# Heads of odd pairs swapped, level 32 on eighths of the array, nine attention phases for thirteen, and one PSUM bank for the first dense product, in a fused linear-attention and MLP kernel

## Chip, cores and metric

One core of a Trainium2 chip. The metric is the device time of one execution in microseconds (us), median over several executions.

Short names in the text: PE is TensorE (the matmul engine), DVE is VectorE, ACT is ScalarE, SP the engine that issues most transfers. PSUM is the memory that matmuls write to; it has eight banks. A quarter of PE's array is 64 rows by 64 columns, an eighth 64 rows by 32 columns. "Changed kernel" is the kernel after the change.

## The reference

A recurrent attention (per head a 48x48 state that decays by `w` and takes up `k v`), followed by a dense block with `h - tanh(h)` between two matrix products:

```python
batch, n_heads, seq, head_dim = (4, 8, 768, 48)
for t in range(S):
    cur = np.einsum('bhd,bhe->bhde', u[None] * kt, vt)
    y[:, :, t] = np.einsum('bhd,bhde->bhe', rt, state + cur)
    state = wt[:, :, :, None] * state + np.einsum('bhd,bhe->bhde', kt, vt)
# x = y as (B*S, 384)
h = x @ w_in            # 384 -> 2048
g = h - np.tanh(h)
return g @ w_out        # 2048 -> 384
```

## The kernel before

The 3072 tokens are cut into eight blocks of 384. Each block's dense part has 16 steps (one per 128 columns of the hidden layer): three matmuls into `hp`, then `h`, `tanh` and a correction series on ACT and DVE, and three steps later three matmuls into `acc`. While the dense steps of block i run, the attention of block i+1 runs between them, one *phase* in a step. Two heads make a pair: head 0 of a pair lies on partitions 0 to 47, head 1 on 64 to 111. Inside a chunk of 64 tokens, scores are computed in levels 1, 2, 4, 8, 16, 32; `update` forms the state at each chunk's start; `result` adds a state part (state times r) and a value part (scores times v).

The dispatch of phases and of the work ahead of them:

```python
        def phase(self, ps, k):
            if k < 2:
                self.level_1(ps, HALVES[k])
                if k == 1:
                    self.decay(1, 0, NPAIR, ("rp",))
            elif k < 7:
                self.level(ps, 2 ** (k - 1), 0, NPAIR)
            elif k < 11:
                p0 = HALVES[(k - 7) // 2]
                if k % 2 == 1:
                    self.turn(ps, p0)
                else:
                    self.update(ps, p0)
            elif k < 13:
                self.result(ps, HALVES[k - 11])
                if k == 12:
                    self.fill_holes([nc.sync])

        def prepare(self, k):

            if k == 10:
                for name, src in (("rmix", rT), ("kmix", kT), ("wt", wT), ("kq", kT)):
                    self.load(name, src, 0, NPAIR)
            elif k == 13:
                self.load("rp", rT, 0, NPAIR)
                self.load_v()
                self.mix(0, NPAIR, False)
                for m in (1, 2, 4, 8, 16, 32):
                    self.totals(m, 0, NPAIR)
            elif k == 14:
                self.decay(1, 0, NPAIR, ("kq",))
```

The result, with its fence between the two parts:

```python
        def result(self, ps, p0, holes_full=False):

            St, rp = states[self.q], self.tiles["rp"]
            yp = ps.tile([P, 2, BANK], F32, name="att", tag="att")
            for p in range(UP):
                for c in range(NCP):
                    for par in range(2):
                        for h in range(2):
                            rows = slice(64 * h, 64 * h + D)
                            t0 = (p0 + p) * NB + (2 * c + par) * L
                            n0 = (p * NCP + c) * L
                            nc.tensor.matmul(yp[64 * h:64 * h + 64, par, n0:n0 + L],
                                             lhsT=St[rows, p0 + p, 2 * c + par, :],
                                             rhs=rp[rows, t0:t0 + L],
                                             start=(p == 0 and c == 0), stop=False,
                                             skip_group_check=True)

            nc.tensor.drain().then_inc(fence, 1)
            fences.append(None)
            nc.tensor.wait_ge(fence, len(fences))
            for p in range(UP):
                for c in range(NCP):
                    for h in range(2):
                        for par in range(2):
                            toks = slice(64 * par, 64 * par + 64)
                            e0 = (p0 + p) * D2 + h * D
                            n0 = (p * NCP + c) * L
                            nc.tensor.matmul(yp[64 * h:64 * h + D, par, n0:n0 + L],
                                             lhsT=self.v[toks, c, e0:e0 + D],
                                             rhs=A[toks, h, p0 + p, c, :],
                                             start=False, stop=(p == UP - 1 and c == NCP - 1),
                                             skip_group_check=True)
            for p in reversed(range(UP)):
                i = p0 + p
                src = yp[:, :, p * NCP * L:(p + 1) * NCP * L].rearrange("e a (c t) -> e c a t", t=L)
                dst = self.xT[:, i, :] if i < KC else self.late
                dst = dst.rearrange("e (c a t) -> e c a t", a=2, t=L)
                for rows in (slice(0, D), slice(64, 64 + D)) if holes_full else (slice(0, P),):
                    nc.scalar.copy(out=dst[rows], in_=src[rows])
```

A level (level 32 is `m == L // 2`; `gram` is a loop of 48 small matmuls, two heads x two halves of the output, so on four quarters of the array):

```python
        def level(self, ps, m, p0, n):
            gr = self.gram(ps, self.tiles["kq"], self.tiles["rp"], p0, n, m, L // 2)
            self.decay(m, p0, n)
            nb = L // (2 * m)
            if m == L // 2:

                for par in range(2):
                    rows = slice(64 * par, 64 * par + 32)
                    dst = A[rows, :, p0:p0 + n].rearrange("s h p c t -> s h (p c) t")
                    nc.scalar.copy(out=dst[:, :, :, 32:],
                                   in_=gr[rows].rearrange("s h (n t) -> s h n t", t=32))
                return
            for h in range(2):
                dst = A[:, h, p0:p0 + n].rearrange("s p c (b two m) -> s (p c) b two m",
                                                   two=2, m=m)[:, :, :, 1, :]
                src = gr[:, h].rearrange("s (n b m) -> s n b m", b=nb, m=m)
                mask = masks[m].bitcast(U8).unsqueeze(1).to_broadcast([P, n * NCP, nb, m])
                nc.vector.copy_predicated(out=dst, mask=mask, data=src)
```

The dense product and the main loop (cut at ...):

```python
    def first(xT, f, ps):
        hp = ps.tile([P, NB], F32, name="hp", tag="hp", bufs=2)
        for kc in range(KC):
            nc.tensor.matmul(hp, lhsT=w_in_sb[:, f, kc, :], rhs=xT[:, kc, :],
                             start=(kc == 0), stop=(kc == KC - 1))
        ...

        for i, blk in enumerate(blocks):
            here = xT
            later = blocks[i + 1] if i + 1 < len(blocks) else None
            after = blocks[i + 2] if i + 2 < len(blocks) else None
            if later:
                xT = later.begin()
            second = Second(blk.b * S + blk.q * NB, ps_d)
            for f in range(NF):
                g, next_rest = first(here, f, ps_d)
                waiting.append((second, f, g))

                for n, op in enumerate(rest):
                    op()
                    if n >= 2 and extra:
                        extra.pop(0)()
                for op in extra:
                    op()
                rest = next_rest
                if later:
                    later.phase(ps_a, f)
                extra = convert(*raws.pop(0)) if raws else []
                if after:
                    after.prepare(f)
                if len(waiting) > LAG:
                    s, fs, gs = waiting.pop(0)
                    s.add(fs, gs)
                if i == 0 and f + AHEAD + RAWS < NF:
                    raws.append(load_weights(f + AHEAD + RAWS, nc.gpsimd))
```

Of the kernel before, what the change touches and what calls it, by code (L numbers as in the profile page):

```python
# [44 lines left out]
P = 128  # L46
L = 64
# [33 lines left out]
def kernel(  # L81
# [88 lines left out]

    fence, fences = tc.alloc_semaphore("fence"), []

    class Block:


        def __init__(self, b, q):
            self.b, self.q = b, q
            self.cols = slice(q * NB, (q + 1) * NB)
            self.tiles = {}
            self.tots = {}  # L180

# [18 lines left out]
        def mix(self, p0, n, copies):  # L200
# [5 lines left out]
            for t, src, odd in ((kmix, kq, 1), (rmix, rp, 0)):  # L206
                if copies:
                    nc.vector.tensor_copy(out=part(t, p0, n, 1 - odd), in_=part(src, p0, n, 1 - odd))
                for p in range(p0, p0 + n):
                    nc.scalar.activation(out=part(t, p, 1, odd),  # L210
                                         in_=part(src if copies else t, p, 1, odd),
                                         func=AF.Copy, scale=u_sb[:, p:p + 1])

        def gram(self, ps, lhs, rhs, p0, n, m, width):

            ps_t = ps.tile([P, 2, BANK], F32, name="att", tag="att")
# [47 lines left out]
        def level(self, ps, m, p0, n):  # L264
            gr = self.gram(ps, self.tiles["kq"], self.tiles["rp"], p0, n, m, L // 2)
            self.decay(m, p0, n)
            nb = L // (2 * m)
            if m == L // 2:

                for par in range(2):  # L270
                    rows = slice(64 * par, 64 * par + 32)
                    dst = A[rows, :, p0:p0 + n].rearrange("s h p c t -> s h (p c) t")
                    nc.scalar.copy(out=dst[:, :, :, 32:],
                                   in_=gr[rows].rearrange("s h (n t) -> s h n t", t=32))
                return
# [6 lines left out]

        def turn(self, ps, p0):

            ks = work.tile([P, UP, NCP, P], F32, name="ks", tag="ks")
            tp = ps.tile([P, 2, BANK], F32, name="att", tag="att")
# [6 lines left out]
            self.ks = ks  # L293

        def update(self, ps, p0):

            ks, last = self.ks, self.q == NQ - 1
            kvp = ps.tile([P, 2, BANK], F32, name="att", tag="att")
# [23 lines left out]
        def result(self, ps, p0, holes_full=False):  # L322

            St, rp = states[self.q], self.tiles["rp"]
            yp = ps.tile([P, 2, BANK], F32, name="att", tag="att")
            for p in range(UP):
                for c in range(NCP):
                    for par in range(2):
                        for h in range(2):
                            rows = slice(64 * h, 64 * h + D)  # L330
                            t0 = (p0 + p) * NB + (2 * c + par) * L
                            n0 = (p * NCP + c) * L
                            nc.tensor.matmul(yp[64 * h:64 * h + 64, par, n0:n0 + L],  # L333
                                             lhsT=St[rows, p0 + p, 2 * c + par, :],
                                             rhs=rp[rows, t0:t0 + L],
                                             start=(p == 0 and c == 0), stop=False,
                                             skip_group_check=True)
# [4 lines left out]
            for p in range(UP):  # L342
                for c in range(NCP):
                    for h in range(2):
                        for par in range(2):
                            toks = slice(64 * par, 64 * par + 64)
                            e0 = (p0 + p) * D2 + h * D
                            n0 = (p * NCP + c) * L
                            nc.tensor.matmul(yp[64 * h:64 * h + D, par, n0:n0 + L],  # L349
                                             lhsT=self.v[toks, c, e0:e0 + D],  # L350
                                             rhs=A[toks, h, p0 + p, c, :],
                                             start=False, stop=(p == UP - 1 and c == NCP - 1),
                                             skip_group_check=True)
            for p in reversed(range(UP)):
                i = p0 + p
                src = yp[:, :, p * NCP * L:(p + 1) * NCP * L].rearrange("e a (c t) -> e c a t", t=L)
                dst = self.xT[:, i, :] if i < KC else self.late
                dst = dst.rearrange("e (c a t) -> e c a t", a=2, t=L)
                for rows in (slice(0, D), slice(64, 64 + D)) if holes_full else (slice(0, P),):
                    nc.scalar.copy(out=dst[rows], in_=src[rows])  # L360
# [10 lines left out]
        def phase(self, ps, k):  # L371
            if k < 2:
                self.level_1(ps, HALVES[k])
                if k == 1:
                    self.decay(1, 0, NPAIR, ("rp",))
            elif k < 7:
                self.level(ps, 2 ** (k - 1), 0, NPAIR)
            elif k < 11:
                p0 = HALVES[(k - 7) // 2]
                if k % 2 == 1:  # L380
                    self.turn(ps, p0)
                else:
                    self.update(ps, p0)
            elif k < 13:
# [190 lines left out]
```

## Time and profile before

| before | value | how to read it |
|---|---|---|
| time | 713.07 us, median of the 3 runs known before the prediction (710.51 to 714.27); a fourth came with the result | span of the profiled run 710.4 us, about 2 us less than its time |
| PE, DVE, ACT busy | 95%, 79%, 69% of the span | averages over boot, block 0 and the rest, which have different bounds |
| boot, to the first dense matmul | 48.74 us | a chain through several engines |
| block 0 | 99.81 us | DVE also converts the weights |
| blocks 1 to 6 | 489.34 us, 81.5 to 81.6 each | PE bound |
| block 7 with the end | 72.51 us | no attention beside it |

The borders are the starts of the first `hp` matmul of each block in PE's order of work. The lines behind these numbers are in the prediction below.

### The profile page before, as it was taken

Reading aid. Unit: us, or ns where it says so; the run is one execution under the profiler, and the core shown is the slowest. Engines: PE = TensorE matmul, PEld = TensorE weight load, DVE = VectorE, ACT = ScalarE, POOL = GpSimd, SP = SyncE. Lnnn points to the kernel's source line nnn. Section 1 sums busy time; section 2 is a strip of 40 time slices with the busy share of each in tenths; the row PEclk is TensorE's granted clock in tenths of the full one; section 3 lists DMA queues with packets and bytes.
Section 4 is the critical chain, followed back from the end, with each engine's and each line's share of the span. In section 5 each row is a group of like instructions: output and inputs, shape, how many; then the busy total and the mean of one; then the engine's idle time right before and its main releaser. Section 6 shows DMA issues by size and latency. Waiting matters only on the chain.

```text
span 710.4 us, 19979 instructions
## 1 busy us (share of the span) xinstructions
PE 675.0 (95%) x8480; PEld 434.6 (61%) x8480; DVE 560.7 (79%) x1125; ACT 487.1 (69%) x957; POOL 10.9 (2%) x32
## 2 busy tenths in 40 slices
PE   4876899999999999999999999999999999999997
PEld 3754555666666666656666666656666566665554
DVE  7778999689876897679876898579976898656774
ACT  4348479586767667586676757686676867677875
POOL 2010000000000000000000000000000000000000
PEclk9987799999999999999999999999999999999999
DMA  8377332213013401114013310124012000000000
GB/s 328 109 266 272 136 128 89 80 43 134 3 47 86 157 14 46 54 36 169 2 46 88 119 52 2 51 82 168 2 46 88 2 35 2 5 7 34 0 0 35
DMA packets 30841, 54.37 MB, mean 77 GB/s; under 512 B 2336, under 2 KB 28704, under 8 KB 30752
## 3 DMA queue, kind: packets, MB, share of 16 engines
q1 hardware_dynamic: 25424, 38.15, 16.3%
q0 software_dynamic: 1872, 10.22, 4.0%
q10 hardware_dynamic: 3456, 4.72, 1.8%
q8 instruction: 67, 1.10, 0.6%
q14 instruction: 22, 0.18, 0.1%
HBM read 47.19 MB, written 4.72 MB: 73 GB/s over the span
## 4 chain that ended last, share of the span: by engine, by line
PE 65%; PEld 11%; DVE 10%; issue 8%; ACT 2%; DMA 2%; PEldq 1%; SPq 1%; ACTq 0%; DVEq 0%
PE acc L471 27%; PE hp L433 25%; PE att L230 10%; PEld hp L433 4%; PEld acc L471 3%; PEld att L333 2%; DVE w_sb L168 2%; PEldq L339 1%; DVE w_sb L166 1%; DVE hs L450 1%; DVE states L318 1%; PE att L349 1%; PE att L290 1%; PE att L308 1%; DMA rp<-in_rT 1%
## 5 line engine op out<-in xcount | busy, mean ns | idle before, releaser
L471 PE MATMUL acc<-w_sb,gT 128*128 128x384 f32 x768 | 279.9, 501 | 0.0
L433 PE MATMUL hp<-xT,w_sb 128*128 128x384 f32 x768 | 273.8, 493 | 3.0 <-DMA xT<-late 3.0
L433 PEld LDWEIGHTS hp<-xT,w_sb 128*128 128x128 f32 x768 | 147.8, 193 | 106.9 <-issue 5.4
L471 PEld LDWEIGHTS acc<-w_sb,gT 128*128 128x128 f32 x768 | 139.9, 191 | 84.4 <-issue 2.3
L440 ACT ACTIVATE h<-hp 128x384 f32<-128x384 f32 x128 | 62.2, 486 | 170.7 <-PE hp L433 168.1
L455 DVE TENSOR_TENSOR th<-h,th 128x384 f32<-128x384 f32 x128 | 70.9, 554 | 56.0 <-ACT th L444 56.0
L450 DVE SCALAR_TENSOR_TENSOR hs<-h,s 128x384 f32<-128x384 f32 x128 | 71.0, 555 | 38.5 <-ACT s L441 37.9
L230 PEld LDWEIGHTS att<-rp,kq 48*64 48x64 f32 x3840 | 68.4, 148 | 30.1 <-issue 28.7
L458 DVE COPY_PREDICATED gT<-big,th 128x384 f32<-128x384 int32 x128 | 76.3, 596 | 12.5 <-ACT qa L442 0.5
L230 PE MATMUL att<-rp,kq 48*64 48x32 f32 x3840 | 72.9, 232 | 10.3 <-issue 5.5
L442 ACT ACTIVATE qa<-s,shift 128x384 f32<-128x384 f32 x128 | 78.7, 615 | 4.2
L450 DVE SCALAR_TENSOR_TENSOR gT<-qb,hs 128x384 f32<-128x384 f32 x128 | 71.3, 557 | 8.5
L445 ACT ACTIVATE big<-s,shift 128x384 f32<-128x384 f32 x128 | 76.8, 600 | 0.0
L443 ACT ACTIVATE qb<-s,shift 128x384 f32<-128x384 f32 x128 | 76.7, 599 | 0.0
L450 DVE SCALAR_TENSOR_TENSOR hs<-qa,hs 128x384 f32<-128x384 f32 x128 | 70.4, 550 | 0.0
L441 ACT ACTIVATE s<-h 128x384 f32<-128x384 f32 x128 | 67.0, 523 | 4.1
L444 ACT ACTIVATE th<-h 128x384 f32<-128x384 f32 x128 | 64.9, 507 | 0.0
L262 DVE TENSOR_TENSOR kq<-kq,tot 128x768 f32<-128x768 f32 (+1 forms) x45 | 38.9, 864 | 10.1 <-PE att L230 9.1
L281 DVE COPY_PREDICATED scores<-mask_all,att 128x384 f32<-128x384 uint8 (+1 forms) x72 | 40.2, 619 | 0.0
L262 DVE TENSOR_TENSOR rp<-rp,tot 128x768 f32<-128x768 f32 (+1 forms) x45 | 38.8, 863 | 0.0
L318 DVE SCALAR_TENSOR_TENSOR states<-states,tot,att 128x48 f32<-128x48 f32 x176 | 32.2, 257 | 6.0 <-PE att L308 6.0
L333 PEld LDWEIGHTS att<-rp,states 48*64 48x64 f32 x768 | 26.0, 146 | 8.9 <-issue 8.9
(47 smaller groups left out, 358.1 us busy)
## 6 DMA issues: line engine op xcount, KB each, us to landing
raw<-in_weights POOLq DMA_DIRECT2D x13, 768.0 KB, 4.6
rmix<-in_rT SPq DMA_DIRECT2D x7, 768.0 KB, 4.5
kmix<-in_kT SPq DMA_DIRECT2D x7, 768.0 KB, 6.1
wt<-in_wT SPq DMA_DIRECT2D x7, 768.0 KB, 8.0
kq<-in_kT SPq DMA_DIRECT2D x7, 768.0 KB, 4.5
rp<-in_rT SPq DMA_DIRECT2D x7, 768.0 KB, 5.9
v_sb<-in_v SPq DMA_DIRECT2D x8, 576.0 KB, 4.1
out_y<-o ACTq DMA_DIRECT2D x24, 192.0 KB, 1.9
```

Source lines behind the costliest of these rows:

```text
L230: nc.tensor.matmul(dst, lhsT=lhs[rows, t0:t0 + L], rhs=src, start=True, stop=True)
L262: nc.vector.tensor_tensor(out=part, in0=part, in1=by, op=ALU.mult)
L433: nc.tensor.matmul(hp, lhsT=w_in_sb[:, f, kc, :], rhs=xT[:, kc, :], start=(kc == 0), stop=(kc == KC - 1))
L441: nc.scalar.activation(out=s, in_=h, func=AF.Square)
L442: nc.scalar.activation(out=qa, in_=s, func=AF.Square, bias=shift[:, 0:1])
L443: nc.scalar.activation(out=qb, in_=s, func=AF.Square, bias=shift[:, 1:2])
L444: nc.scalar.activation(out=th, in_=h, func=AF.Tanh)
L445: nc.scalar.activation(out=big, in_=s, func=AF.Relu, bias=shift[:, 2:3])
L450: return lambda: nc.vector.scalar_tensor_tensor(out=out, in0=in0, scalar=scalar, in1=in1, op0=op0, op1=ALU.mult)
L455: lambda: nc.vector.tensor_tensor(out=th, in0=h, in1=th, op=ALU.subtract),
L458: lambda: nc.vector.copy_predicated(out=g, mask=big.bitcast(I32), data=th)]
L471: nc.tensor.matmul(acc, lhsT=g[:, j * P:(j + 1) * P], rhs=w_out_sb[:, f, :], start=(f == 0), stop=(f == NF - 1))
```

## The change

Its intent is to take matmul time off PE where PE is the bound:

- **State part on four quarters.** In odd pairs the two heads are swapped in the output, so that head 0's rows meet the other half of the columns. Even and odd pairs then use different quarters and run at once. The rows of `w_in` are permuted on the host to match.
- **Level 32 on eighths.** Only 32 of the 64 keys are of use there, so two pairs share a column half as two tiles of 64 rows x 32 columns.
- **Nine phases for thirteen.** Both halves of level 1, turn, update and result go into one phase each; the scratch pool in PSUM has two tiles for one.
- **One `hp` bank** (`hp` is the output of the first dense product), which pays for the second scratch tile (a scratch tile takes two banks, the three accumulators three).
- **u on DVE.** The multiplication of k and r by u goes from ACT (eight operations) to DVE (two), and all work ahead is spread over steps 10 to 15. In block 0 the phases start at step 3.

The core of the diff. The state part:

```diff
-        def result(self, ps, p0, holes_full=False):
+        def result(self, ps, pairs, holes_full=False):
             St, rp = states[self.q], self.tiles["rp"]
-            yp = ps.tile([P, 2, BANK], F32, name="att", tag="att")
-            for p in range(UP):
+            yp = [scratch(ps) for e in range(2)]
+            slots = [pairs[n:n + 2] for n in range(0, len(pairs), 2)]
+            for n, slot in enumerate(slots):
                 for c in range(NCP):
                     for par in range(2):
-                        for h in range(2):
-                            rows = slice(64 * h, 64 * h + D)
-                            t0 = (p0 + p) * NB + (2 * c + par) * L
-                            n0 = (p * NCP + c) * L
-                            nc.tensor.matmul(yp[64 * h:64 * h + 64, par, n0:n0 + L],
-                                             lhsT=St[rows, p0 + p, 2 * c + par, :],
-                                             rhs=rp[rows, t0:t0 + L],
-                                             start=(p == 0 and c == 0), stop=False,
-                                             skip_group_check=True)
+                        for p in slot:
+                            for h in range(2):
+                                rows = slice(64 * h, 64 * h + D)
+                                e0 = 64 * (h ^ (p % 2))
+                                t0 = p * NB + (2 * c + par) * L
+                                n0 = (n * NCP + c) * L
+                                nc.tensor.matmul(yp[p % 2][e0:e0 + 64, par, n0:n0 + L],
+                                                 lhsT=St[rows, p, 2 * c + par, :],
+                                                 rhs=rp[rows, t0:t0 + L],
+                                                 start=(n == 0 and c == 0), stop=False,
+                                                 skip_group_check=True)
```

Level 32:

```diff
+        def last_level(self, ps, p0, n):
+            half, m = n // 2, L // 2
+            ps_t = scratch(ps)
+            used = ps_t[:, :, 0:half * NCP * m].rearrange("s h (p c t) -> s h p c t", p=half, c=NCP)
+            for p in range(half):
+                for c in range(NCP):
+                    for h in range(2):
+                        for par in range(2):
+                            for w in range(2):
+                                t0 = (p0 + w * half + p) * NB + (2 * c + par) * L
+                                rows = slice(64 * h, 64 * h + D)
+                                s0 = 64 * par + 32 * w
+                                nc.tensor.matmul(used[s0:s0 + m, h, p, c, :],
+                                                 lhsT=self.tiles["kq"][rows, t0:t0 + m],
+                                                 rhs=self.tiles["rp"][rows, t0 + m:t0 + L],
+                                                 start=True, stop=True)
+            for par in range(2):
+                for w in range(2):
+                    s0 = 64 * par + 32 * w
+                    at = slice(p0 + w * half, p0 + w * half + half)
+                    dst = A[64 * par:64 * par + m, :, at].rearrange("s h p c t -> s h (p c) t")
+                    nc.scalar.copy(out=dst[:, :, :, m:],
+                                   in_=used[s0:s0 + m].rearrange("s h p c t -> s h (p c) t"))
```

The multiplication by u, and the plan of phases that takes the place of the numbered dispatch:

```diff
+            elif name in ("kmix", "rmix"):
+                t = self.tiles[name].rearrange("d (p n two) -> d p n two", p=NPAIR, two=2)
+                t = t[:, :, :, 1 if name == "kmix" else 0]
+                nc.vector.tensor_tensor(out=t, in0=t, op=ALU.mult,
+                                        in1=u_sb.unsqueeze(2).to_broadcast([P, NPAIR, NB // 2]))
...
+    def plan(i):
+        names = ("level 1", 2, 4, 8, 16, 32, "turn", "update")
+        first_step = 3 if i == 0 else 0
+        phases = {first_step + n: name for n, name in enumerate(names)}
+        result = first_step + len(names) + 1
+        phases[result] = "result"
+        prep = {}
+        def put(f, block, *what):
+            prep.setdefault(f, []).extend((block, name) for name in what)
+        if i == 0:
+            put(0, 1, "kmix", "rmix")
+            put(1, 1, "totals 1", "kq")
+            put(2, 1, "totals 2", "rp")
+        put(first_step + 1, i + 2, "load 1")
+        put(first_step + 7, i + 2, "load 2")
+        put(result + 1, i + 2, "load 3")
+        for f, name in zip(range(NF - 6, NF), ("kmix", "rmix", "totals 1", "totals 2", "kq", "rp")):
+            put(f, i + 2, name)
+        return phases, prep
...
-        hp = ps.tile([P, NB], F32, name="hp", tag="hp", bufs=2)
+        hp = ps.tile([P, NB], F32, name="hp", tag="hp")
...
-    ps_a = ctx.enter_context(tc.tile_pool(name="ps_a", bufs=1, space=PSUM))
+    ps_a = ctx.enter_context(tc.tile_pool(name="ps_a", bufs=2, space=PSUM))
...
+    def head(n):
+        return n ^ (n // 2 % 2)
```

## The prediction

> **What bounds the kernel now.** I read the page's shares and slices first, then the busy time of each engine in stretches cut at the block borders, then the order of work on TensorE inside one block, and last VectorE and ScalarE in the same stretch.
>
> ```profile
> PE 675.0 (95%) x8480; PEld 434.6 (61%) x8480; DVE 560.7 (79%) x1125; ACT 487.1 (69%) x957; POOL 10.9 (2%) x32
> PE   4876899999999999999999999999999999999997
> DVE  7778999689876897679876898579976898656774
> ```
>
> TensorE (PE) has little idle time after the first sixth. The kernel has eight blocks of 16 dense steps; while block i's dense steps run, the attention of block i+1 runs in between. Cut at the first dense matmul of the blocks (engine columns: busy us and instructions of PE, PEld, DVE, ACT, POOL):
>
> ```profile
> 0.00:48.70 48.70, 31.35 (x876) 29.13 (x876) 38.75 (x102) 21.14 (x38) 6.13 (x23) 1.00 0.64 224
> 48.70:100.00 51.30, 40.40 (x638) 25.90 (x639) 46.04 (x77) 34.42 (x59) 3.70 (x7) 0.80 0.56 201
> 100.00:148.55 48.55, 46.70 (x397) 28.82 (x397) 40.91 (x87) 37.77 (x74) 1.05 (x2) 0.97 0.25 81
> 148.55:230.10 81.55, 81.34 (x1069) 51.86 (x1068) 65.55 (x133) 57.06 (x116) 0.00 (x0) 1.00 0.21 66
> 638.00:710.40 72.40, 68.28 (x211) 39.39 (x209) 44.66 (x84) 52.84 (x105) 0.00 (x0) 1.00 0.05 17
> ```
>
> There are four regimes. Boot (48.7 us) is a chain through several engines. Block 0 (99.9 us) is longer than the others because VectorE (DVE) also converts the weights; from 56 to 127 us the chain of waits lists DVE lines almost alone, so DVE is the bound there. Blocks 1 to 6 take 489.5 us together, 81.6 each, and PE is busy for 81.34 of 81.55: a pure PE bound, DVE at 80%, ScalarE (ACT) at 70%. The last block has no attention beside it. So a saving on PE counts in full in blocks 1 to 6, six times, until DVE's 65.5 us or ACT's 57 us is reached.
>
> PE's order of work, block 1 (start us, length us, group; a run's length includes a pipeline tail, so I take differences of starts):
>
> ```profile
> 138.88 2.10 PE L471 MATMUL acc<-w_sb,gT 128*128 128x384 f32 x6
> 140.81 2.10 PE L433 MATMUL hp<-xT,w_sb 128*128 128x384 f32 x6
> 142.75 2.10 PE L471 MATMUL acc<-w_sb,gT 128*128 128x384 f32 x6
> ...
> 155.51 0.93 PE L230 MATMUL att<-rmix,kmix 48*64 48x64 f32 x48
> 156.37 2.20 PE L471 MATMUL acc<-w_sb,gT 128*128 128x384 f32 x6
> 158.41 2.10 PE L433 MATMUL hp<-xT,w_sb 128*128 128x384 f32 x6
> 160.43 1.60 PE L230 MATMUL att<-rp,kq 48*64 48x32 f32 x96
> 161.97 2.20 PE L471 MATMUL acc<-w_sb,gT 128*128 128x384 f32 x6
> 164.00 2.10 PE L433 MATMUL hp<-xT,w_sb 128*128 128x384 f32 x6
> ...
> 205.28 2.10 PE L433 MATMUL hp<-xT,w_sb 128*128 128x384 f32 x6
> 207.31 1.61 PE L333 MATMUL att<-rp,states 48*64 48x64 f32 x48
> 209.01 0.89 PE L349 MATMUL att<-scores,v_sb 64*48 64x64 f32 x48
> 209.83 2.20 PE L471 MATMUL acc<-w_sb,gT 128*128 128x384 f32 x6
> 211.87 2.10 PE L433 MATMUL hp<-xT,w_sb 128*128 128x384 f32 x6
> ```
>
> A bare dense step is 142.75 - 138.88 = 3.87 us. A level step is 164.00 - 158.41 = 5.59, so the phase costs 1.72: 1.53 of small matmuls and 0.2 for the two changes of form (hp to att 2.03 against 1.94 us, acc to hp 2.04 against 1.94). The result step is 211.87 - 205.28 = 6.59, or 2.72 extra: state part 1.70 with its drain, value part 0.82, changes 0.2.
>
> The key number is time per quarter of the array. Each fp32 matmul shows as two instructions. Level 1: 0.86 us for 48 over four quarters, 12 each, 72 ns per instruction and quarter. State part: 1.70 us for 48, but head h uses rows and columns of its own half, so two quarters with 24 each: 71 ns. Same cost per quarter, half the quarters used. The update takes 0.84 us with 48 instructions (192.96 to 193.80) and 0.83 with 40 (274.56 to 275.39), when one chunk drops out and only two quarters get shorter: so the fullest quarter sets the time, not the issue rate.
>
> **What the Trainium skill says.** "TensorEngine Tiling (Array Packing)", section Key Properties: tiles run load and matmul independently, and changing the mode drains the engine. The trace agrees: the 71 to 72 ns per quarter, and the 0.1 us at each change. "TensorE: Matmul & The Clock Gate", section Part 3: Packing small matmuls, has tiles starting about 4 ns apart; Part 1 of the page ("Wait — 56ns, not 53.3ns?") gives a floor of about 25 ns from start to start. The trace differs from the second: 1.53 us for 96 instructions is 16 ns each. With 4 ns each for load and matmul, 8 ns a pair is my estimate of the issue limit. "PSUM — Partial Sum Buffer", section PSUM bank collisions raise a hardware error, says row tiles may not write one bank at once; this is why the swapped odd pairs get their own two banks. With two scratch tiles (four banks) and three accumulators, one of the eight banks (Specifications) is left for hp.
>
> **The change, part by part (per block, blocks 1 to 6).**
> State part: 96 instructions on four quarters, 24 each at 71 ns: 1.70 instead of 3.40 us. The value part stays at 48 + 48 on four quarters: 0.82 + 0.84. The result phases cost 2 x 2.72 = 5.44 now; then 1.70 + 1.66 + 0.2 = 3.56. Saved: 1.88.
> Level 32: 96 instructions over eight tiles, 12 each instead of 24, with a load of 32 columns instead of 64. At 64 ns per tile (1.53 us / 24) or a little under it is 0.69 to 0.77 us; the issue limit (96 x 8 ns) also gives 0.77. I take 0.80 for 1.53. Saved: 0.73.
> Merged phases: level 1 twice 1.06 and update twice 1.04 lose one pair of changes each: 0.2 + 0.2. Turn works on the full array and shows no change cost (0.66 each), so nothing. Saved: 0.40.
> Sum 3.0 us per block, 78.6 for 81.6; six blocks: **-18.0 us**.
> DVE beside it: u is now multiplied on DVE, two operations over 128x768 elements, about 0.87 us from start to start like kq<-kq,tot (173.54 to 174.40): 65.5 + 1.7 = 67.3 of 78.6, hidden. ACT loses eight activations (3.1 us at 142.10 to 145.00) and gains two small copies. In the busiest step (update, both halves) DVE has 2.66 dense + 2 x 2.11 = 6.9 us against PE's 5.8; an empty step follows and g is needed only three steps later.
> One hp bank: hp(f+1) now waits for ACT's copy of hp(f). In a bare step hp ends at 139.04, the copy runs 139.08 to 139.57, the next hp starts at 140.81: 1.2 us spare. Only a backlog on ACT eats that, and the largest one now is the mix, which moves away. I allow **+0.5** for the output copies at the start of the last block.
> Boot: PE runs at half pace there (six transposes take 1.54 us, later 0.82). Level 32 saves some 1.3 us and the first result's state part (2.80 us) 1.4 before the late DMA can start: **-2.7**.
> Block 0: the DVE-bound stretch ends with the last update at 125.6. It starts 2.7 earlier (counted above), gains 1.7 (mix) and about 1.3 (totals that now fill a DVE gap at 46 to 50 us come later): +3.0. After that PE took 148.55 - 125.6 = 22.9 us; now the two dense runs before the result are already done, and there are left one result 3.56 and seven dense runs of 1.94, 17.2 with changes: -5.7. Block 0: **-2.7** net.
> Last block: no change. Total 713.07 - 18.0 + 0.5 - 2.7 - 2.7 = 690.2; I say 690.
>
> **Rivals.** (a) The quarters don't overlap as counted, because the load of a tile has to wait for matmuls in the same rows. Against: the level form already runs four quarters. If so, the state part saves nothing: 7 x 1.7 = 12 us lost, 702. (b) Level 32 is held by issue at 16 ns an instruction: +0.73 x 6, about 695. (c) The single hp bank stalls PE, by a late ACT copy in steps with phase copies (turn: ACT 4.5 of 5.2 us; level 32: 4.8 of 4.7): half a us in three steps of each block is +10, 700. For it: ACT is in order, and level 32 now has four copies. Against: the spare 1.2 us. (d) DVE or latency becomes the bound in the merged update or in block 0, so that block 0 gains nothing or loses: +3 to +8, 693 to 698. None leads to a slower kernel alone.
>
> **Range and chances.** Everything as counted, with a level 32 at 0.7 and a better block 0, gives 685; one of (b) and (d) gives 693 to 698. 80%: 684 to 699. Faster by over 2% means under 698.8. That takes the state part and no new steady wait: 0.87. Within 2%: 0.11. Slower: 0.02.
>
> **What would show each step.** Right: blocks 1 to 6 at 78.6 us; state part 96 instructions in about 1.7 us and the value part in 1.65; level 32 in 0.7 to 0.8; bare steps still 3.87; first dense matmul at about 46 us, block 1 starting near 143. Wrong: the state part over 2.5 us (a); level 32 above 1.2 (b); waits of hp for ACT's h, or bare steps over 3.9 (c); idle PE in front of the result or of levels, released by DVE (d).

## The result, and the profile after

| | before | changed |
|---|---|---|
| median us | 712.16 (4 runs, 710.51 to 714.27) | 690.65 (4 runs, 690.1 to 690.94) |
| ratio | 1 | 0.9695, 95% interval 0.9666 to 0.9725 |
| span of the profiled run | 710.4 | 688.1 |

A ratio here is the mean time of one kernel's fast runs over that of the other's fast runs of the same rounds, so not quite the ratio of the medians quoted.

The page of the changed kernel, part 1 and two rows of the 40 slices:

```profile
PE 648.3 (94%) x8480; PEld 414.8 (60%) x8480; DVE 567.4 (82%) x1139; ACT 472.5 (69%) x919; POOL 10.9 (2%) x32
PE   4766789999999999999999999999999999999997
DVE  7788999999869897789879897698878898566764
```

PE lost 26.7 us of busy time with as many matmuls (8480) as before: nothing was removed from PE, the same instructions were packed more tightly. DVE gained 6.7 us, ACT lost 14.6.

The stretches of the changed kernel, cut at the block borders (columns: length, then busy us and instructions of PE, PEld, DVE, ACT, POOL, then granted clock, DMA share, GB/s):

```profile
47.46:143.94 96.48, 82.43 (x1035) 50.72 (x1035) 90.84 (x170) 70.74 (x128) 4.77 (x9) 0.90 0.43 151
143.94:222.91 78.97, 78.42 (x1069) 50.00 (x1068) 67.27 (x136) 55.02 (x110) 0.00 (x0) 1.00 0.21 69
301.15:379.40 78.25, 78.11 (x1069) 49.84 (x1068) 66.51 (x135) 55.02 (x110) 0.00 (x0) 1.00 0.22 69
379.40:458.78 79.38, 78.42 (x1054) 50.00 (x1052) 65.86 (x131) 55.02 (x110) 0.00 (x0) 1.00 0.21 68
615.24:688.10 72.86, 68.66 (x211) 39.40 (x209) 44.65 (x84) 52.96 (x105) 0.00 (x0) 0.99 0.05 17
```

Four of the blocks 1 to 6 take 78.2 us with PE busy for all but 0.14 us: still a pure PE bound. Two of them, 1 and 4, are longer by 0.7 and 1.1 us; that was not predicted, and the experiments go into it. The ledger:

| stretch | before | changed | difference | predicted |
|---|---|---|---|---|
| boot | 48.74 | 47.46 | -1.3 | -2.7 |
| block 0 | 99.81 | 96.48 | -3.3 | -2.7 |
| blocks 1 to 6 | 489.34 | 471.30 | -18.0 | -18.0 |
| block 7 and end | 72.51 | 72.86 | +0.35 | +0.5 |
| sum | 710.4 | 688.1 | -22.3 | -22.9 |

PE's order of work in block 3 of the changed kernel (start us, length us, group), to be held against the lines of the prediction:

```profile
329.18 2.10 PE L476 MATMUL hp<-xT,w_sb 128*128 128x384 f32 x6
331.20 1.02 PE L298 MATMUL att<-rp,kq 48*32 48x32 f32 x96
332.16 2.20 PE L514 MATMUL acc<-w_sb,gT 128*128 128x384 f32 x6
334.20 2.10 PE L476 MATMUL hp<-xT,w_sb 128*128 128x384 f32 x6
...
348.86 2.10 PE L476 MATMUL hp<-xT,w_sb 128*128 128x384 f32 x6
350.89 1.63 PE L364 MATMUL att<-rp,states 48*64 48x64 f32 x96
352.65 1.56 PE L382 MATMUL att<-scores,v_sb 64*48 64x64 f32 x96
354.14 2.20 PE L514 MATMUL acc<-w_sb,gT 128*128 128x384 f32 x6
356.18 2.10 PE L476 MATMUL hp<-xT,w_sb 128*128 128x384 f32 x6
```

The state part of all four pairs takes 352.65 - 350.89 = 1.76 us, as much as it took for two pairs before. The result step is 356.18 - 348.86 = 7.32 us, 3.45 over a bare one. Level 32 takes 0.95 us (0.96 by the rounded starts above) instead of 1.53, its step 5.02.

In the last block the single bank shows at the one place where ACT is busy with the output copies (the changed kernel; before, the `hp` run that starts at 653.87 came 2.43 us after the `acc` run of 651.44, which waits for the same copies):

```profile
628.79 2.60 PE L514 MATMUL acc<-w_sb,gT 128*128 128x384 f32 x6
631.43 2.20 PE L476 MATMUL hp<-xT,w_sb 128*128 128x384 f32 x6
```

Here it comes 2.64 us after, and its own run is followed 2.04 us later instead of 1.93: together the 0.3 us of this block.

### The profile page after: what moved, and what is told of

The parts are those of the page before. It is cut to its first block, busy times and chain, and to the rows that moved or that the text cites. A ratio compares the mean times of both kernels' runs of the same rounds, so it can differ in the third digit from the quotient of the medians.

```text
span 688.1 us, 19930 instructions
## 1 busy us (share of the span) xinstructions
PE 648.3 (94%) x8480; PEld 414.8 (60%) x8480; DVE 567.4 (82%) x1139; ACT 472.5 (69%) x919; POOL 10.9 (2%) x32
## 3 DMA queue, kind: packets, MB, share of 16 engines
q8 instruction: 66, 1.08, 0.6%
## 4 chain that ended last, share of the span: by engine, by line
PE 73%; DVE 12%; issue 5%; PEld 4%; ACT 3%; DMA 2%; SPq 1%; PEldq 1%; ACTq 0%; DVEq 0%
PE acc L514 31%; PE hp L476 29%; PE att L235 9%; DVE states L345 2%; PE att L382 2%; DVE w_sb L171 2%; PEld hp L476 2%; PE att L317 2%; PEld att L364 1%; DVE w_sb L169 1%; DVE hs L493 1%; PEld acc L514 1%; DVE rp L267 1%; DVE kq L267 1%; PE att L298 1%
## 5 line engine op out<-in xcount | busy, mean ns | idle before, releaser
L514 PEld LDWEIGHTS acc<-w_sb,gT 128*128 128x128 f32 x768 | 142.0, 192 | 90.0 <-issue 2.4
L485 ACT ACTIVATE qa<-s,shift 128x384 f32<-128x384 f32 x128 | 78.8, 615 | 4.2
L235 PEld LDWEIGHTS att<-rp,kq 48*64 48x64 f32 x3072 | 55.0, 148 | 27.6 <-issue 16.7
L235 PE MATMUL att<-rp,kq 48*64 48x32 f32 x3072 | 58.7, 231 | 11.5 <-DVE scores L242 4.9
L235 PE MATMUL att<-rmix,kmix 48*64 48x64 f32 x768 | 14.5, 232 | 8.6 <-ACT rmix L216 7.2
```

The source lines that it names most:

```text
L235: nc.tensor.matmul(dst, lhsT=lhs[rows, t0:t0 + L], rhs=src, start=True, stop=True)
L485: nc.scalar.activation(out=qa, in_=s, func=AF.Square, bias=shift[:, 0:1])
L514: nc.tensor.matmul(acc, lhsT=g[:, j * P:(j + 1) * P], rhs=w_out_sb[:, f, :], start=(f == 0), stop=(f == NF - 1))
```

## The experiments

The theory: PE bounds blocks 1 to 6, and the gain there is the sum of four-quarter state parts, eighths in level 32 and fewer runs of small matmuls; the single bank costs next to nothing as long as ACT is never late. Rivals: the gain of the result comes from the merging rather than the quarters; the bank costs something; the rest is in block 0 alone. Twelve kernels ran, all but one with a correct result. Their diffs are shortened here, and words after # in them are notes.

| run | what is other than in the changed kernel | median us | ratio to before (95%) | a block of 1 to 6, us |
|---|---|---|---|---|
| e1 | heads not swapped | 700.29 | 0.9821 (0.9802 to 0.9839) | 79.6 |
| e2 | level 32 on quarters | 695.16 | 0.9748 (0.9728 to 0.9767) | 78.8 |
| e3 | level 1, turn, update split again | 694.49 | 0.9744 (0.9723 to 0.9766) | 78.9 |
| e4 | *before*, with one hp bank | 719.21 | 1.0088 (1.0065 to 1.0111) | 82.5 |
| e5 | u on ACT | 690.77 | 0.9687 (0.9658 to 0.9716) | 78.3 |
| e6 | level 32, rows alternate | 690.18 | 0.9682 (0.9654 to 0.9709) | 78.25 |
| e7 | level 32, 16 columns (wrong result) | 689.8, one run | - | 78.22 |
| e8 | load of v ahead of rp | 690.22 | 0.9682 (0.9656 to 0.9708) | 78.25 |
| e9 | block 0 starts at step 1 | 688.50 | 0.9654 (0.9626 to 0.9683) | 78.25 |
| e10 | SP's queue in program order | 690.63 | 0.9682 (0.9653 to 0.9710) | 78.25 |
| e11 | result in two phases | 693.44 | 0.9721 (0.9691 to 0.9752) | 78.9 |
| e12 | block 0 starts at step 0 | 688.94 | 0.9665 (0.9643 to 0.9686) | 78.25 |

The last column is the usual length of a block in that run's trace, without the blocks that have a pause (1 and 4; in e3 3 and 4; in e10 also 2). The other block lengths repeat within 0.1 us, so they tell more than the whole time, where the boot alone differs by 2 us from run to run (first dense matmul at 46.8 to 48.9 us in the traces of the changed kernel and its variants, 50.2 in e4).

### e1: the swap undone

```diff
-                                e0 = 64 * (h ^ (p % 2))
+                                e0 = 64 * h          # both parts
-        return n ^ (n // 2 % 2)
+        return n
```

> The changed kernel, but the odd pairs keep their heads unswapped, so the state part runs on two quarters again; all else (merged phases, two banks a parity, level 32 on eighths) stays. Theory of quarters: the state part takes about 3.45 us instead of 1.77 (48 instructions a quarter at 71 to 74 ns), blocks 1 to 6 take 79.9 us instead of 78.25, and the whole is 11 to 13 us slower than the changed kernel: 702 to 704 us. Rival (the gain of the result step comes from the merging, not from the quarters): state part near 1.8 us, 690 to 692 us.

PE's order in the result step of block 2 of this run:

```profile
277.56 3.01 PE L364 MATMUL att<-rp,states 48*64 48x64 f32 x96
280.69 1.56 PE L382 MATMUL att<-scores,v_sb 64*48 64x64 f32 x96
282.18 2.20 PE L514 MATMUL acc<-w_sb,gT 128*128 128x384 f32 x6
```

The state part takes 3.13 us on two quarters and 1.77 on four: the swap is worth 1.36 us a block, and with it the rival falls. But 3.13 is less than the 3.45 I expected: 48 instructions in a quarter are not 48 x 71 ns. Before, a run with 24 in a quarter took 1.70; 24 more cost 1.43 us, or 60 ns each, and 0.27 us is paid once per run (the drain at the fence is in it). The 71 ns of the prediction were 60 ns and a share of a fixed cost. Block time 79.6 for 78.25, where 79.9 was expected, and 9.6 us in the whole: 700.3 us, short of the 702 to 704 expected. The value part of block 1 takes 1.88 us here, and block 4 has no pause.

### e2: level 32 back on quarters

```diff
-            if m == L // 2:
-                self.last_level(ps, p0, n)
-                self.decay(m, p0, n)
-                return
             gr = self.gram(ps, self.tiles["kq"], self.tiles["rp"], p0, n, m, L // 2)
+            # level 32: two copies on ScalarE, as before
```

> The changed kernel, but level 32 as before: all four pairs on quarters, two copies on ScalarE. Theory: the phase goes from 0.95 back to 1.53 us, a level 32 step from 5.02 to 5.60, six blocks +3.5, block 0 and boot another +0.5 to +2: 694.5 to 696.5 us. Rival (level 32 is hidden by something else, such as the vector engine's decays): 690 to 691.5 us.

Level 32 takes 1.53 us again and an undisturbed block 78.83 instead of 78.25, as expected; the whole is 4.5 us slower. In the traces the six blocks together are 4.4 us longer: 3.5 by level 32, the rest by longer pauses in blocks 1 and 4 (80.26 and 80.14 us, for 78.97 and 79.38).

### e3: level 1, turn and update split into two phases again

```diff
+        if i > 0:
+            names = tuple(("level 1", p) for p in HALVES) + (2, 4, 8, 16, 32) + tuple(
+                (what, p) for p in HALVES for what in ("turn", "update"))
```

> The changed kernel, but from block 1 on level 1, turn and update are split into two phases each again, as before (result stays merged). If a phase costs only its two changes of form, 0.2 us, this adds 0.4 us a block, +2.4 us, 693 us. If the profile after is right that merging saved 0.36 on level 1 and 0.34 on update, it adds 0.7 a block, +4.2 us, 695 us. Turn should cost the same either way (1.31 against 2 x 0.66).

(The load of `kq` moves three steps later with it.) The second number was right: 78.94 us a block, 0.69 more, and 3.8 us in the whole. The pauses are in blocks 3 and 4 here (80.10 and 79.86 us). Why merging is worth more than the changes of form shows in a split step of this run:

```profile
303.78 0.93 PE L235 MATMUL att<-rmix,kmix 48*64 48x64 f32 x48
304.64 2.20 PE L516 MATMUL acc<-w_sb,gT 128*128 128x384 f32 x6
```

Level 1 of two pairs takes 0.86 us, of all four in one run 1.56, not 1.72. So 12 instructions more in each quarter cost 0.70 us, 58 ns each, and 0.16 us is paid per run, beside the 0.2 for the changes. Turn came out the same either way (0.65 and 1.31).

### e4: the kernel before with one hp bank

```diff
-        hp = ps.tile([P, NB], F32, name="hp", tag="hp", bufs=2)
+        hp = ps.tile([P, NB], F32, name="hp", tag="hp")
```

> The kernel before with one hp bank instead of two and nothing else. Theory: a bank alone costs only where ScalarE is late, and that is after the eight u activations of step 13: the hp that started at 144.68 must wait for a copy that ends at 145.46, so about 0.8 us in each of 7 blocks and 0.35 at the start of the last, +5 to +6.5 us, 717 to 719 us. If one bank costs nothing: 712 to 713 us. If it costs in every phase step: over 725 us.

It costs 6.9 us (719.21 against 712.30 us), a little more than the 5 to 6.5 expected, and at the expected place, after ACT's eight u operations (PE's order of work):

```profile
147.76 2.20 PE L433 MATMUL hp<-xT,w_sb 128*128 128x384 f32 x6 [0.65 <-ACT h L440]
230.24 2.20 PE L433 MATMUL hp<-xT,w_sb 128*128 128x384 f32 x6 [0.67 <-ACT h L440]
```

Blocks 1 to 5 take 82.5 instead of 81.55 us each: the late run starts 0.8 us after its place and is itself 0.1 longer. Block 6, which has nothing to prepare, takes 81.5. In no other step of these blocks does PE wait for the bank. The first line shown is of block 0, so about half of what block 0 loses (101.58 for 99.81) is the same wait; for the other half, and for a boot that is 1.4 us longer in this trace, the cause is not shown.

### e5: u on ScalarE in the changed kernel

```diff
-                nc.vector.tensor_tensor(out=t, in0=t, op=ALU.mult, in1=...)
+                for p in range(NPAIR):
+                    nc.scalar.activation(out=t[:, p], in_=t[:, p], func=AF.Copy, scale=u_sb[:, p:p + 1])
```

> The changed kernel, but u is multiplied on ScalarE again (four activations each at steps 10 and 11, 1.5 us each step). My reading: in bare steps ScalarE has 3.0 of 3.87 us, so its copy of hp comes 0.65 us late after step 10 and 1.3 us late after step 11, and the spare before the next hp is 1.2 us: a stall of 0 to 0.15 us a block, 690 to 692 us. Rival: one bank and the mix on ScalarE don't go together, as in the kernel before with one bank (0.67 us of stall a block and 0.93 us a block in all): 695 to 697 us.

690.77 us, blocks of 78.30: 0.06 us a block, nothing in the whole. So with the plan of the changed kernel, in which k and r have a step each, u could have stayed on ACT. Together with e4 this speaks for the lump of eight operations in one step, not the engine, as what the single bank can't bear.

### e6 and e7: what holds level 32 at 0.95 us

e6 turns the loops so that consecutive matmuls take different row halves; e7 streams half of the columns, with a wrong result.

```diff
-                    for h in range(2):
-                        for par in range(2):
-                            for w in range(2):
+                    for par in range(2):
+                        for w in range(2):
+                            for h in range(2):
```

```diff
-                                nc.tensor.matmul(used[s0:s0 + m, h, p, c, :],
+                                nc.tensor.matmul(used[s0:s0 + m, h, p, c, 0:16],   # rhs and copies too
```

> The changed kernel, with the order inside level 32 turned so that each matmul takes the other half of the rows than the one before. If level 32 (0.95 us for 96 instructions, 8.2 ns each after 0.16 fixed) is held by the issue of instructions, it stays at 0.95 us. If it is held by matmuls of the same rows waiting for each other, it falls to 0.75 to 0.85. Time of the whole 690 +- 1 either way; the profile decides.

> Wrong result on purpose: level 32 streams 16 columns instead of 32, with as many instructions. Issue bound: 0.95 us again. Bound by the work of each eighth: 0.80 to 0.90 us.

e6: 0.95 us, so the order of rows is not it. e7, level 32 of block 3:

```profile
331.55 1.00 PE L298 MATMUL att<-rp,kq 48*32 48x16 f32 x96
332.48 2.20 PE L514 MATMUL acc<-w_sb,gT 128*128 128x384 f32 x6
```

0.93 us: 16 columns fewer save 0.02. That looks like the issue bound, but it does not settle it, because on quarters the columns hardly matter either (level 1 with 64 columns 1.56 us, a level with 32 columns 1.53, both 24 instructions in a quarter). With the 0.16 us per run taken off, level 32 has 66 ns per instruction and eighth, or 8.2 ns per instruction overall; on quarters it is 58 ns. Either the issue of pairs of load and matmul holds it at about 8 ns each, or an eighth needs 66 ns per instruction whatever it streams. This stays open.

### e8 and e10: the pauses in blocks 1 and 4

In the changed kernel, PE's order shows a pause inside the value part of blocks 1 and 4, always at the same instruction (the 85th of the 96 in block 1, the 94th in block 4, also in e2, e5, e6, e8 and e10), with no releaser, that is, with nothing in the profile that it waited for:

```profile
197.30 0.43 PE L382 MATMUL att<-scores,v_sb 64*48 64x64 f32 x12 [0.41 <-issue]
433.28 0.31 PE L382 MATMUL att<-scores,v_sb 64*48 64x64 f32 x3 [0.82 <-issue]
```

The first suspicion was the load of `rp` for the block after next: it is issued at 195.36 us, when the state part has released `rp`, and 768 KB then run beside PE's instruction fetch.

```diff
-                self.load("rp", rT, 0, NPAIR)
-                self.load_v()
+                self.load_v()
+                self.load("rp", rT, 0, NPAIR)
```

> The changed kernel, with the load of v issued ahead of the load of rp, so that the rp load can't start before the value part has ended. Theory: the two pauses of 0.7 and 1.1 us in the value parts of blocks 1 and 4 come from PE's instruction fetch waiting behind the rp load, which starts as soon as the state part has released rp; then they go, blocks 1 and 4 take 78.25 us like the others, 1.8 us off in all: 688.5 to 689.5 us. Rival (the fetch can't keep up with 192 short matmuls in a row whatever the other transfers do): the pauses stay, 690 to 691 us.

The run is a failed experiment: the pauses stayed (0.47 and 0.87 us), but in block 1 the `rp` load was still issued first, at 196.74, in the middle of the result, because SP's queue is ordered by the scheduler and not by the program. So it tells nothing about the load. e10 forces the order:

```diff
-    with tc.manual_schedule(engines={PE, DVE, ACT}):
+    with tc.manual_schedule(engines={PE, DVE, ACT, mybir.EngineType.SP}):
```

> The try with v first did not do what it should: the rp load still started right after the state part, since the order of the sync queue was left to the scheduler. Here that queue is kept in program order, so rp and v load after the value part and after the late rows. If the pauses in the value parts of blocks 1 and 4 come from the rp load, they go: all six blocks 78.25 us, 1.2 to 1.9 us off. If the instruction stream itself runs dry, the pauses stay and the time too, 690 to 691 us.

Now `rp` is issued at 203.98 us, after the result. The pauses stay, 0.47 and 1.00 us. The stretches around the first one (length, PE busy, granted clock, DMA share, GB/s):

```profile
195.80:196.00 0.20, 0.20 (x16) 1.00 0.30 82
...
197.20:197.40 0.20, 0.20 (x25) 1.00 0.00 0
197.40:197.60 0.20, 0.20 (x12) 1.00 0.00 0
197.60:197.80 0.20, 0.00 (x0) 1.00 0.00 0
197.80:198.00 0.20, 0.00 (x0) 1.00 0.00 0
198.00:198.20 0.20, 0.13 (x9) 1.00 0.00 0
```

From 195 to 200 us the only transfers are two packets of the instruction queue, 0.03 MB together; one of them moves at 195.8. PE stops at 197.6. The load of `rp` is ruled out as the cause. A new pause of the same kind (0.66 us, no releaser) turned up at 244.88 us, in a level of block 2, seven instructions before the end of its 96, while output rows were being written. The profiled run was the slowest of the five, 692.07 us; the median is 690.63, as in the changed kernel.

### e11: the result in two phases

```diff
+        if i > 0:
+            phases[result], phases[result + 1] = "result a", "result b"
```

> The changed kernel, from block 1 on with the result in two phases of two pairs each, still on four quarters. Theory that 192 short matmuls in a row drain the instruction stream: no pauses with 96 in a row. Cost of the split from the fixed 0.41 of a state run (with its drain), 0.15 of a value run and 0.2 of the changes: 2 x (1.09 + 0.82 + 0.2) = 4.2 instead of 3.45 us, +0.75 us a block, 79.0 us each, no block longer, about 693 us. If the pauses stay, two blocks are longer than the others by 0.7 to 1.1 us.

All six blocks take 78.90 to 78.93 us, none is longer, and no pause is left. The two state parts take 1.04 to 1.07 us (12 in a quarter; 24 take 1.77, again 60 ns each). Together with e10 this speaks for the instruction stream: the "Trainium skill", page "Runtime: NRT & Kernel Launch", section Instruction fetch mechanics, has it that an engine's instructions come in blocks of 16 KiB, 256 instructions, and that crossing into the next is mostly hidden. The trace agrees with the size (66 packets for 1.08 MB on the instruction queue). A merged result is 384 instructions, loads and matmuls, in 3.3 us, so it uses up more than a block in one go; where a border falls badly, the next block of instructions isn't there in time.

The traces can be asked further, by counting all of PE's records in order (matmuls, loads, its drains and semaphore waits). Every pause of over 0.25 us in blocks 1 to 6 then sits at the same place of a stretch of 256: e10's three start at records 5825, 6849 and 12226, which leave 193, 193 and 194 when divided by 256, and e3's, in other blocks, at 10178 and 12226 (194 both). Packets of the instruction queue and such borders can be paired off in order. In each of these pauses PE goes on 1.2 to 1.6 us after the end of its packet, and at none of 912 borders in all fourteen traces does it go on sooner than 1.2 us after. In e10 the packet that moves at 195.87 is the one that the first pause waits for: it has landed by 196.82, and PE goes on at 198.07. So the pauses are waits for the next block of instructions: e10's first comes without any data transfer beside it, all sit at the borders and end within a narrow time after the packet, and those in the result go when the run is halved. Why the packet of just these borders starts late stays open. A run of 96 is no full guard, as e10's pause in a level shows.

In the changed kernel the pauses cost 1.85 us, less than what e11's split costs (0.68 us in each of six blocks).

### e9 and e12: when block 0's phases start

```diff
-        first_step = 3 if i == 0 else 0
+        first_step = 1 if i == 0 else 0      # e9, all preparations of block 1 at step 0
+        first_step = 0                       # e12, all preparations ahead of the loop
```

> The changed kernel, but in block 0 the phases start at step 1 instead of 3, with all preparations of block 1 at step 0. The vector engine is busy for 90.8 of block 0's 96.5 us, so little can be won: its last update comes two dense steps of work earlier (about 9.7 us), the matmul tail behind it is two steps longer (7.7 us): block 0 94 to 97 us, the whole 688 to 691 us. If the late start was what made block 0 shorter than before, it is 3 us or more longer.

> The changed kernel, but block 0 has its phases from step 0 like all others, with block 1's preparations ahead of the loop. Starting at step 1 made block 0 94.8 us instead of 96.5. If that gain comes from a shorter matmul tail behind the last wait for the vector engine (112.2 us in the changed kernel, 102.1 with step 1), one step more is worth another 0.5 to 1.5 us, and preparations that fill the vector engine's idle 4 us near 50 us may add 1 to 2: block 0 92 to 94.5 us, the whole 685.5 to 688.5 us. If it was chance of the boot, 690 us.

Block 0 takes 94.78 us (e9) and 94.22 (e12); with the start at step 3 it took 95.9 to 96.7 in the changed kernel and eight of the nine variants of it (98.9 in e1). The last wait of PE for DVE in block 0, in the changed kernel first and then in e9:

```profile
112.23 1.53 PE L317 MATMUL att<-ident,kq 128*128 128x128 f32 x12 [1.17 <-DVE kq L267]
```

```profile
102.12 1.53 PE L317 MATMUL att<-ident,kq 128*128 128x128 f32 x12 [1.16 <-DVE kq L267]
```

Both are the turn phase. What follows is PE bound: 143.94 - 112.23 = 31.7 us there, 141.57 - 102.12 = 39.5 us in e9. Counted from the start of block 0 (47.46 and 46.79 us), the part up to this wait gets 9.4 us shorter (64.8 to 55.3), the tail 7.7 longer. e9 and e12 have the lowest medians of all, 688.5 and 688.9 us, 2 us (0.3%) below the changed kernel's 690.65. They were run at other times. The intervals of the ratios overlap; that block 0 is shorter by 1.7 to 2.3 us is what the traces show. e10, of the same call as e9 and with the start at step 3, took 689.95 to 692.07 us, e9 687.91 to 689.04, so about 2 us is likely. e12 was expected at 685.5 to 688.5 us and missed that by 0.4.

## Why the prediction was right, point by point

The time was predicted at 690.0 us and is 690.65, with the bound as predicted. Step by step:

| step (one block of 1 to 6) | predicted | measured | shown by |
|---|---|---|---|
| state part | -1.70 | 3.43 to 1.77: -1.66 | trace; e1: 1.36 of it by the swap, the rest by merging |
| value part | +0.02 | 1.64 to 1.49: -0.15 | trace |
| changes of form in the result | -0.2 | -0.2 | result step 3.45 over a bare one, for 5.44 |
| level 32 | -0.73 | -0.58 | e2 |
| merged level 1 and update | -0.40 | -0.70 | e3 |
| sum | -3.0 | -3.3 | 81.55 to 78.25 |
| pauses | none | +0.7 and +1.1, in two blocks | e10, e11 |

- **PE as the bound** of blocks 1 to 6 held: bare steps are still 3.87 us, PE idles 0.14 of 78.25 us, and each part that was undone came back in full (e1, e2, e3).
- **The time per quarter** was mis-sized, in the prediction's words "72 ns per instruction and quarter". It is 58 to 60 ns, and 0.16 us (0.27 with the drain) per run of small matmuls. The difference divides a run's time by its instructions as if nothing were fixed. It made the merging too cheap (0.2 us a pair of phases for 0.34 to 0.36) and level 32 too good, since its 0.95 us also has the fixed part in it.
- **The pauses** were in no part of the sum and in no rival. That the six blocks came out at -18.0 us as predicted is luck, two errors that cancel: 0.3 us a block better, 1.85 us of pauses.
- **Level 32** landed between the counted 0.80 and rival (b). The estimate of 8 ns a pair for the issue fits what was measured once the fixed 0.16 us is taken off, but e7 can't tell it from a fixed time per eighth.
- **The single bank**, rival (c): no wait in blocks 1 to 6, 0.35 us in the last block for the 0.5 allowed. But the prediction looked for it in blocks 1 to 6 and the last alone. In block 0, steps 1 to 3, `hp` waits for ACT's `h` three times, 5.2 us in all; before the longest wait (line below) and the 0.71 us after it, ACT's trace has two weight conversions just ahead of that copy. In e9 0.6 us of this is left, in e12 nothing; what it costs beside the DVE bound of block 0 was not tried apart. e4 shows that the rival was real for a kernel with the lump of u operations. The prediction took u's move to DVE as what pays for the bank; e5 shows that spreading it over two steps is enough.
- **DVE**, rival (d): no wait for it from the turn of block 0 on, which is busy for 67.3 us at most of a block of 78.2 to 79.4.
- **Block 0** came close (-3.3 for -2.7), but for another reason than the one told. The prediction has the DVE bound end with the last update; in the trace it ends at the turn, at 112.2 us, and the result starts at 127.0 without a wait. That the number came close is luck; what made block 0 shorter was not tried apart. The late start at step 3 was no gain, as e9 and e12 show.
- **Boot** gained 1.3 us for 2.7. The traces with the same boot start the first dense matmul anywhere from 46.8 to 48.8 us, so the whole of this term isn't resolved. Its parts can be read in the trace: the first state part takes 1.64 us for 2.89, about as counted (1.4), but the first transposes start at 30.45 us for 30.84, so of the 1.3 us counted for level 32 at most 0.4 is gained; PE waits 0.5 and 0.3 us for DVE's decays there.
- **Banks of their own** for the swapped odd pairs, for which the prediction names a rule on PSUM: no run here tried it without.

The longest wait for the single bank in block 0 of the changed kernel:

```profile
58.97 3.88 PE L476 MATMUL hp<-xT,w_sb 128*128 128x384 f32 x6 [3.85 <-ACT h L483]
```

## What to carry to other kernels

When a run of small matmuls is spread over tiles of the array, fit its time as a fixed part and a time per instruction of the fullest tile, from two runs of different length, before counting what a merge or a split is worth. Look for idle tiles first: filling the two idle quarters was the largest single gain here, with no instruction removed. A single-buffered PSUM bank cost nothing in the steps of blocks 1 to 6 here, and 0.9 us a block with a lump of ACT's work in one step (e4); look at that engine's other work, and try to spread it over steps before moving it to another engine. If PE stops in a long run of short matmuls and waits for nothing, count its records from pause to pause: differences near multiples of 256 pointed to the instruction fetch here.

## What the Trainium skill lacked or had wrong

- "TensorE: Matmul & The Clock Gate", Part 1: the floor of about 25 ns from start to start is given without saying that it does not hold across tiles, for which Part 3 of the same page has about 4 ns. A level on quarters has 96 matmul instructions in 1.53 us, 16 ns each, and level 32 on eighths 96 in 0.95 us, 9.9 ns each, loads of the weights included.
- The same page gives no time for fp32 load and matmul pairs that follow each other in one tile. Here they take 58 to 60 ns per instruction in a quarter and some 66 in an eighth, plus 0.16 us per run, and the streamed columns hardly count (64 or 32: 1.56 or 1.53 us; 32 or 16: 0.95 or 0.93 us).
- "TensorEngine Tiling (Array Packing)", Key Properties, says that a change of mode drains the engine but not what it costs: about 0.1 us at each change here (2.03 for 1.94 us, 2.04 for 1.94), and no such cost for a full-array transpose.
- "Runtime: NRT & Kernel Launch", Instruction fetch mechanics, calls the crossing of a 16 KiB border mostly hidden. Of six results, each of 192 short matmul instructions and as many loads, two had pauses that add 0.7 and 1.1 us to their blocks, which went when the run was halved. They sit at borders of 256 records, and PE goes on 1.2 to 1.6 us after the packet that it waited for.
